# Sums moved off GpSimd in a fused attention and gated-layer kernel: the out projection's sums of h go to VectorE and ahead of their stage, its sums of C to accumulating DMAs

## The chip, the cores and the metric

One core of one Trainium2 chip. The metric is the device time of one execution in microseconds (us); lower is better. Three runs of the kernel before are given, and one further execution was profiled.

## The reference, cut to what matters

```python
def phi(x):                                   # x: 8 batches, 8 heads, 576 positions, 64
    h = einsum('bhsd,md->bhsm', x, omega) - sum(x*x, -1)/2
    return exp(h - max(h, -1)) / sqrt(128)
q_p, k_p = phi(q * 64**-0.25), phi(k * 64**-0.25)
kv  = einsum('bhsm,bhsd->bhmd', k_p, v);  z = sum(k_p, axis=2)
att = einsum('bhsm,bhmd->bhsd', q_p, kv) / (einsum('bhsm,bhm->bhs', q_p, z)[..., None] + 1e-6)
x   = att.transpose(0, 2, 1, 3).reshape(4608, 512)
xn  = x / sqrt(mean(x*x, -1) + 1e-6) * rms_g
g   = xn @ w_gate;  val = xn @ w_val          # 512 -> 1536
out = (silu(g) * val) @ w_out                 # the out projection, 1536 -> 512
```

The change concerns the last product. There h = silu(g) * val, turned so that its 1536 features lie on partitions in twelve tiles of 128 (f = 0 to 11) and its 4608 tokens along the free axis in nine blocks of 512.

## The kernel before, in words

**Stages.** Attention and normalisation come first, mixed with the gate and value products of the first three feature tiles. Then the "units" make the other nine feature tiles of h in two passes (`PASSES`); each finished 128x512 piece of h is stored to DRAM (`h_scratch`). In the second pass the blocks 6, 7 and 8 are served first (`TURNS`). The last stage is the out projection.

**The out projection in 15 products.** The nine token blocks are taken as three triples, `TRIPLES = ((6, 7, 8), (0, 1, 2), (3, 4, 5))`, called triple 0, 1 and 2 here. For a triple the work is one block product C = A B, where A is w_out cut in 2 x 3 blocks, B is h cut in 3 x 3 blocks b(j, l) (j a third of the features, that is four tiles; l a token block), and C has 2 x 3 blocks c(i, l). A bilinear scheme (`PRODUCTS`, `MADE`) makes C from 15 products where the plain way needs 18. The left operands are sums of blocks of A, made once. The right operands are sums of blocks of h, named e1 to e13 and f3: 13 sums for each triple, of which 11 are operands; e1 and e8 are only steps. For example e1 = b11 + b21, e2 = b01 - e1. The other four operands are plain blocks b. Each product's result is added to or subtracted from one or two blocks of C, 18 such readings for a triple (a "sum of C" below).

Each right operand has four feature tiles and is handled in two halves of two tiles, g = 0 and g = 1, each 128 x 1024 numbers. The loads `hb<-h_scratch` fetch a half (512 KB). A sum of h is one instruction `hb<-hb,hb` (or `he`) on 128x1024. Before the change the sums with g = 0 run on VectorE (DVE) and those with g = 1 on GpSimd (POOL):

```python
by = "POOL" if g else "DVE"
made[nm, g] = add(by, ..., form(nm, g, host, ve if by == "DVE" else nc.gpsimd), ...)
```

**Three passes for one product.** TensorE (PE) works on numbers split in a high and a low part. `halve` casts the high part on ScalarE (ACT), `hR3h<-hb`, and makes the remainder by a subtraction, `hR3l<-hb,hR3h`, on DVE (the number is that of the product, 0 to 14). The weights are split in the same way, `oh<-oraw` and `ol<-oraw,oh`, 30 halves in all, once; `oraw` comes from `wl_scratch`. Products 0 to 3 have theirs early; of the products 4 to 14 the half g = 1 has its `ol` on POOL. A product is 2 halves x 2 output tiles (u = 0, 1) x 6 matmuls of 128x512, which makes 24, and the stage 45 x 24 = 1080.

**Slots and chains.** The split operands lie in five slots (`SLOTS_R`) that are used in turn, so that half i can be cast when PE is done with half i - 5. The results are held in PSUM in seven chains; a chain that several products add to (as chain 4: products 5 and 7; chain 6: products 3, 6, 8, 11) may go on only when the earlier reading of it is done. The first reading of each block of C is a copy on ACT (`c<-q`, L1588 or L1586), each later one an addition on DVE (`c<-c,q`, L1590 and L1592), into a tile of the pool `acc` (up to nine); after the last one SP stores the tile to `out_dram`. `hb` has up to eleven buffers.

**Order.** A planner (`Plan`) simulates all instructions with estimated costs and keys and writes them out in one fixed order for each engine; each engine works through its own list in that order and waits at the head for what is not ready. SP's list holds all DMA issues, loads and stores alike.

Of the kernel before, what the change touches and what calls it, by code (L numbers as in the profile page):

```python
# [9 lines left out]
F32 = mybir.dt.float32  # L10
# [11 lines left out]
P = 128  # L22
# [58 lines left out]
    "first": {f"hb{i}": (1, 1) for i in range(8)},  # L81
    "ahead": {"k6": (1, 1), "k7": (1, 1), "k8": (1, 1), "wa": (1, 1)},
    "last": {"wo": (1, 1)},
}
# [3 lines left out]
    "hb": ("raw", 11),  # L88
# [25 lines left out]
)  # L114
WHERE = LONE + tuple(x[0] for x in LEFT)
# [185 lines left out]
def performer_glu_kernel(  # L301
# [14 lines left out]
    wl_d: bass.AP,  # L316
):
# [25 lines left out]
    def leave(group):  # L343
        stacks.pop(group).close()
# [988 lines left out]

    base = 6000
    for ps, units in enumerate(PASSES):
        if ps == len(PASSES) - 1:
            for n in range(EARLY, 3 * NF):
# [5 lines left out]
                ["ahead", "products"],  # L1343
# [17 lines left out]
    in_c = change(list(range(to_c)), ["products"], ["last"])  # L1361
# [3 lines left out]
    def out_weights(n, key):  # L1365
# [28 lines left out]
        for g in range(KT // 2):  # L1394
# [9 lines left out]
            for k in range(2) if n in (0, 12) else (None,):  # L1404
# [4 lines left out]
                else:  # L1409
# [6 lines left out]
                        "POOL" if n > 3 and g == 1 else "DVE", lambda o=out: o("h"),  # L1416
# [8 lines left out]
    def out_right(tr, key):  # L1425
# [3 lines left out]
        need = []  # L1429

        def want(nm):
            if nm in need:
                return
            if nm in MADE:
                want(MADE[nm][0])
                want(MADE[nm][2])
            need.append(nm)

        steps = []
        for n, (_, nm, _, _) in enumerate(PRODUCTS):  # L1440
            want(nm)
            steps += [x for x in need if x not in [y for y, _ in steps]] and [
                (x, None) for x in need if x not in [y for y, _ in steps]
            ]
            steps.append((nm, n))
        last = {}
        for at, (nm, n) in enumerate(steps):
            for x in (nm,) if n is not None or nm not in MADE else (nm, MADE[nm][0], MADE[nm][2]):
                last[x] = at

        def load(nm, g):
            def go():
                j, l = int(nm[1]), int(nm[2])
                t[nm, g] = tile_("hb", [P, 2, TB], f"h{nm}_{tr}_{g}")
# [5 lines left out]
        def form(nm, g, host, eng):  # L1460
            def go():
# [5 lines left out]
                eng.tensor_tensor(  # L1467
# [31 lines left out]
        soon = {}  # L1499
        for at, (nm, n) in enumerate(steps):  # L1500
            if n is None:
                soon[nm] = next(m for x, m in steps[at:] if m is not None)
        for at, (nm, n) in enumerate(steps):
            for g in range(KT // 2):
                if n is not None:
                    readers[nm, g].append(halves(n, g, nm))
                elif nm not in MADE:
                    j, l = int(nm[1]), int(nm[2])
                    f, c0 = KT * j + 2 * g, blocks[l] * TB
                    after = [  # L1510
                        i
                        for key_, i in st.items()
                        if key_[0] == "hs" and key_[1] in (f, f + 1)
                        and key_[2] < c0 + TB and key_[2] + key_[3] > c0
                    ]
                    token[nm, g] = ("hb", tr, nm, g)
                    takes.append(token[nm, g])
                    made[nm, g] = add(
                        "SP", TB / 977 / RATE, load(nm, g), after + [to_c],
                        key + 4 * soon[nm] + 2 * g - 1 + 0.01 * at, [token[nm, g]], land=LATER,  # L1520
                    )
                    readers[nm, g] = []
                else:
                    x, _, y = MADE[nm]
                    host = next((z for z in (x, y) if last[z] == at), None)
                    after = [made[x, g], made[y, g]]
                    take = []
                    if host is None:
                        token[nm, g] = ("hb", tr, nm, g)
                        takes.append(token[nm, g])  # L1530
                        take = [token[nm, g]]
                    else:
                        token[nm, g] = token.pop((host, g))
                        after += readers[host, g]
                    by = "POOL" if g else "DVE"
                    made[nm, g] = add(
                        by, 0.09 + TB / 485 if by == "DVE" else 0.25 + TB / 240,
                        form(nm, g, host, ve if by == "DVE" else nc.gpsimd),
                        after, key + 4 * soon[nm] + 2 * g - 0.5 + 0.01 * at, take,
                    )  # L1540
                    readers[x, g].append(made[nm, g])
                    readers[y, g].append(made[nm, g])
# [183 lines left out]
```

## Time and profile before

| | before |
|---|---|
| median of 3 runs | 1068.82 us (1068.14 to 1071.82) |
| the profiled execution's own time | 1072.78 us |
| its span in the profile | 1070.9 us |
| busy shares of the span | PE 96%, DVE 85%, ACT 60%, POOL 29% |
| granted PE clock, mean | 0.986 of full speed (2.4 GHz) |

The span runs from the first to the last instruction of the profiled execution. Matmuls are pipelined, so that a matmul's own duration (389 ns) is longer than the distance between two of them. "Idle" of an engine names the instruction that ended the wait.

### The profile page before, as it was taken

What the parts mean: (1) busy time and instruction counts of PE and PEld (TensorE: products, weight loads), DVE (VectorE), ACT (ScalarE), POOL (GpSimd) and SP (SyncE); (2) the same over time, 40 slices, a digit from 0 to 9 for tenths busy, and PEclk for the clock granted to TensorE, in tenths of its full rate; (3) what the DMA queues carried; (4) which work ended last, traced back from release to release, by engine and by line L of the source; (5) the groups of instructions that cost most, each with busy time, mean ns of one, the idle gap of its engine ahead of it and who ended that gap; (6) DMA issues with size and microseconds to landing.
All of it is one profiled execution on the core that took longest, in us unless ns stands there. A gap on an engine that the chain in (4) does not pass through costs nothing.

```text
span 1070.9 us, 20656 instructions
## 1 busy us (share of the span) xinstructions
PE 1030.0 (96%) x7645; PEld 872.2 (81%) x7645; DVE 911.9 (85%) x1447; ACT 647.3 (60%) x1443; POOL 314.6 (29%) x305
## 2 busy tenths in 40 slices
PE   9999999999999999999999999999998789989988
PEld 7889888888888888888897889888886668768766
DVE  5899899988887575989899677686799999999996
ACT  6999989899786465554555366445454344334431
POOL 1233212212222355000234250000156544353450
PEclk9999999999999999999999999999999989989998
DMA  7877676766543675755577464332444643453222
GB/s 250 267 235 240 216 240 217 216 207 203 165 164 109 196 227 167 272 200 187 199 239 227 155 209 139 121 118 102 174 160 125 220 168 120 142 175 118 87 91 78
DMA packets 109924, 191.37 MB, mean 179 GB/s; under 512 B 9216, under 2 KB 51968, under 8 KB 109824
## 3 DMA queue, kind: packets, MB, share of 16 engines
q1 hardware_dynamic: 109824, 190.06, 54.1%
q8 instruction: 60, 0.98, 0.4%
q14 instruction: 40, 0.33, 0.1%
HBM read 126.71 MB, written 63.31 MB: 177 GB/s over the span
## 4 chain that ended last, share of the span: by engine, by line
PE 65%; DVE 16%; ACT 6%; issue 5%; DMA 2%; POOL 0%; SPq 0%; DVEq 0%; ACTq 0%; POOLq 0%
PE pa L295 6%; PE pa L296 6%; PE pa L297 6%; PE q L296 4%; PE q L297 4%; PE q L295 4%; PE ff L295 4%; PE ff L297 4%; PE ff L296 4%; PE pb L296 3%; PE pb L295 3%; PE pb L297 3%; PE nu L842 2%; PE pjq L667 2%; PE pc L296 2%
## 5 line engine op out<-in xcount | busy, mean ns | idle before, releaser
L1467 POOL TENSOR_TENSOR hb<-hb,hb 128x1024 f32<-128x1024 f32 x33 | 97.5, 2957 | 243.0 <-DVE c L1273 123.4
L1291 ACT ACTIVATE c<-c 128x512 f32<-128x512 f32 (+1 forms) x90 | 52.8, 589 | 108.9 <-DVE c L1273 108.5
L295 PE MATMUL ff<-xhi,whi 128*128 128x512 f32 (+3 forms) x248 | 94.5, 381 | 1.5 <-ACT qpT L834 0.5
L911 POOL TENSOR_TENSOR xlo<-xr,xhi 128x256 fp32r<-128x256 f32 x72 | 55.4, 792 | 135.4 <-ACT xhi L908 135.3
L297 PE MATMUL ff<-xhi,wlo 128*128 128x512 f32 (+3 forms) x248 | 90.4, 365 | 0.0
L296 PE MATMUL ff<-xlo,whi 128*128 128x512 f32 (+3 forms) x248 | 90.3, 364 | 0.0
L697 ACT ACTIVATE qp<-pjq,biq 128x128 f32<-128x128 f32 x288 | 79.7, 411 | 16.4 <-DVE biq L688 16.3
L697 ACT ACTIVATE kp<-pjk,bik 128x128 f32<-128x128 f32 x280 | 78.6, 433 | 4.0 <-DVE bik L688 3.3
L1467 DVE TENSOR_TENSOR hb<-hb,hb 128x1024 f32<-128x1024 f32 x33 | 58.6, 1780 | 3.2 <-DMA hb<-h_scratch 2.7
L1273 DVE TENSOR_TENSOR c<-pb,u 128x512 f32<-128x512 f32 (+1 forms) x45 | 28.4, 633 | 36.2 <-PE pb L297 30.2
L295 PEld LDWEIGHTS ff<-xhi,whi 128*128 128x128 f32 x248 | 46.7, 188 | 10.3 <-ACT xr L898 0.9
L680 DVE TENSOR_REDUCE mxq<-pjq 128x4 f32<-128x512 f32 x72 | 46.6, 682 | 8.3 <-PE pjq L667 8.3
L297 PEld LDWEIGHTS ff<-xhi,wlo 128*128 128x128 f32 x248 | 46.7, 188 | 7.7
L548 POOL TENSOR_TENSOR sr<-w,w 128x256 f32<-128x256 f32 x16 | 13.9, 898 | 129.8 <-DVE w L446 129.1
L296 PEld LDWEIGHTS ff<-xlo,whi 128*128 128x128 f32 x248 | 46.8, 189 | 6.2
L680 DVE TENSOR_REDUCE mxk<-pjk 128x4 f32<-128x512 f32 x72 | 46.5, 682 | 6.0 <-PE pjk L667 6.0
L834 ACT COPY qpT<-qt 128x512 f32<-128x512 f32 x72 | 40.3, 644 | 2.7 <-PE qt L831 2.7
L667 PE MATMUL pjk<-front,ink 64*128 64x128 f32 x576 | 39.5, 279 | 1.5 <-issue 1.4
L667 PE MATMUL pjq<-front,inq 64*128 64x128 f32 x560 | 39.4, 281 | 0.5 <-DVE rec L856 0.4
L842 PEld LDWEIGHTS nu<-kv,qpT 128*64 128x64 f32 x1152 | 35.9, 137 | 4.7 <-issue 1.9
L667 PEld LDWEIGHTS pjk<-front,ink 64*128 64x128 f32 x576 | 35.5, 190 | 5.1 <-issue 2.6
L842 PE MATMUL nu<-kv,qpT 128*64 128x65 f32 x1152 | 39.5, 223 | 0.1
(289 smaller groups left out, 3383.4 us busy)
## 6 DMA issues: line engine op xcount, KB each, us to landing
hb<-h_scratch SPq DMA_DIRECT2D x54, 512.0 KB, 4.4
h_scratch<-c SPq DMA_DIRECT2D x72, 256.0 KB, 2.2
ink<-in_kx_dram SPq DMA_DIRECT2D x32, 512.0 KB, 4.9
inq<-in_qx_dram SPq DMA_DIRECT2D x32, 512.0 KB, 4.6
Xb<-xn_scratch SPq DMA_DIRECT2D x28, 512.0 KB, 4.9
f<-in_wgv_dram SPq DMA_DIRECT2D x24, 512.0 KB, 4.6
xn_scratch<-xr SPq DMA_DIRECT2D x36, 256.0 KB, 3.0
out_dram<-c SPq DMA_DIRECT2D x36, 256.0 KB, 2.1
```

The source lines that it names most:

```text
L295: nc.tensor.matmul(out, lhsT=ah, rhs=bh, start=first, stop=False, skip_group_check=again)
L296: nc.tensor.matmul(out, lhsT=ah, rhs=bl, start=False, stop=False, skip_group_check=again)
L297: nc.tensor.matmul(out, lhsT=al, rhs=bh, start=False, stop=last, skip_group_check=again)
L667: nc.tensor.matmul(t["pts"][i][:, hp, :], lhsT=x[rows, hp, :], rhs=om[rows, :], start=hp == 0 or not first, stop=True, skip_group_check=first,
L680: ve.tensor_reduce(out=by_half[:, i, :], in_=t["pts"][i], axis=AX.X, op=ALU.max)
L697: nc.scalar.activation(st[tag + "p", c][:, h, :], t["pts"][h % 2][:, h // 2, :], AF.Exp, bias=t["bi"][:, h : h + 1], scale=SCALE,)
L834: nc.scalar.copy(t["qpT"][:, 4 * half : 4 * half + 4, :], t["pt", half])
L842: nc.tensor.matmul(pt[lo:hi, i, :], lhsT=t["qpT"][:, h, lo:hi], rhs=st["kv", b][:, h, :], start=True, stop=True,)
L911: nc.gpsimd.tensor_tensor(out=st["xT", blk][1][:, ccs, cs], in0=t["xr"][:, ccs], in1=st["xT", blk][0][:, ccs, cs].bitcast(F32), op=ALU.sub ...
L1273: ve.tensor_tensor(out=t[name], in0=t[bank], in1=t[y], op=ALU.add)
L1291: nc.scalar.activation(t[nm], t[nm], AF.Silu)
L1467: eng.tensor_tensor(out=t[nm, g], in0=t[x, g], in1=t[y, g], op=ALU.add if sign == "+" else ALU.subtract,)
```

## The change

What the change does, in five parts.

1. **No GpSimd in the out projection's sums.** The 39 sums of h that POOL made, the 13 with g = 1 of each triple, are now on DVE. The 11 weight remainders `ol` with g = 1 go to DVE too.
2. **Half of triple 0's sums in the unit stage.** `staged` makes the 13 sums for the feature tiles f = 0 and 1 of each third (that is g = 0) during the second pass: 18 loads `sb<-h_scratch`, 26 sums of 128x512 on DVE and 22 stores to a new DRAM tensor `f_scratch`. In the out projection these 11 operands come by one load each (`he<-f_scratch`) and need no sum.
3. **Sums of C added in DRAM.** In triples 1 and 2, blocks of C listed in `APART` are not summed in SBUF: a reading becomes a copy on ACT into a tile of its own; the first tile is stored by SP, the following ones are sent by a DMA that POOL issues and that adds to what DRAM holds (`accum_op=ALU.add`). Such a DMA waits until the previous one on the same tile of C has landed. In triple 1 all readings of c01, c11, c02, c10 and the first of c00 and c12 are apart; in triple 2 all of c01, c11, c02 and the first of c10. In triple 0 nothing changes in this.
4. **Buffers.** `fs`, nine tiles of 128x512, serves part 2 while the units run; three of the eight later `hb` buffers therefore open only after the units' last instruction.
5. The planner's order follows from all this. PE has the same 4838 rows in the same sequence.

Counted over the whole program: DVE sums of h 39 -> 65 of 128x1024 and 0 -> 26 of 128x512; DVE sums of C 72 -> 38; ACT copies of C 36 -> 70; POOL sums of h 39 -> 0, POOL `ol` 12 -> 0, POOL DMAs 0 -> 34 of 256 KB; `hb` and `he` loads 54 -> 60.

```diff
+EARLY_F = (0, 1)
+FORMS = ("e1", "e2", "f3", "e4", "e12", "e5", "e6", "e7", "e8", "e9", "e10", "e11", "e13")
+TOLD = tuple(x for x in FORMS if x in [p[1] for p in PRODUCTS])
+APART = ({}, {"c01": 3, "c11": 3, "c02": 3, "c10": 3, "c00": 1, "c12": 1}, {"c01": 3, "c11": 3, "c02": 3, "c10": 1})
...
+    def staged(after, key):
+        blocks = TRIPLES[0]
+        for f in EARLY_F:
...
+                    ve.tensor_tensor(
+                        out=t[nm], in0=t[x], in1=t[y], op=ALU.add if sign == "+" else ALU.subtract
+                    )
...
+                return lambda: nc.sync.dma_start(f_d[TOLD.index(nm), :, f], t[nm])
...
+        if ps == len(PASSES) - 1:
+            staged(again, base - 16)
...
-                        "POOL" if n > 3 and g == 1 else "DVE", lambda o=out: o("h"),
+                        "DVE", lambda o=out: o("h"),
...
+            forms = {} if tr == 0 and 2 * g in EARLY_F else MADE
...
+                if nm in MADE:
+                    nc.sync.dma_start(t[nm, g], f_d[TOLD.index(nm), :, 2 * g : 2 * g + 2])
+                    return
...
-                    by = "POOL" if g else "DVE"
...
+                made[nm, g] = add(
+                    "DVE", 0.09 + TB / 452, form(nm, g, host), after, here - 0.5, take
+                )
...
+                if onto:
+                    nc.gpsimd.dma_start(to, t[nm, u], accum_op=ALU.add)
+                else:
+                    nc.sync.dma_start(to, t[nm, u])
...
+                    nth = [m for m, _ in parts[nm]].index(n)
+                    alone = APART[tr].get(nm, 0)
+                    begin = nth <= alone
+                    end = nth < alone or n == parts[nm][-1][0]
...
+                        onto = (nm, u) in sent
+                        sent[nm, u] = add(
+                            "POOL" if onto else "SP", 1.0 if onto else TB / 1950 / RATE,
+                            store(nm, u, onto), [sums[nm, u]] + ([sent[nm, u]] if onto else []),
+                            top, give=[("acc", tr, nm, u, begun[nm, u])], land=LATER if onto else LAND,
+                        )
```

**Place 1: DVE in triple 1, around product 8.** In the names the first number after the tile is the triple, the next is g (for `c` and `q` it is u); the long number is a buffer's. Before:

```order
L1110 TENSOR_TENSOR hR7l_0_11538<-hb_1_0_11028,hR7h_0_11537 128x1024
L1467 TENSOR_TENSOR he_1_0_11560<-hb_1_0_11391,hb_1_0_11364 128x1024
L1110 TENSOR_TENSOR hR7l_1_11558<-hb_1_1_11055,hR7h_1_11557 128x1024
L1110 TENSOR_TENSOR hR8l_0_11584<-hb_1_0_11157,hR8h_0_11583 128x1024
L1110 TENSOR_TENSOR hR8l_1_11602<-hb_1_1_11195,hR8h_1_11601 128x1024
L1592 TENSOR_TENSOR c_1_0_11366<-c_1_0_11366,q_1_0_11453 128x512
L1592 TENSOR_TENSOR c_1_1_11376<-c_1_1_11376,q_1_1_11467 128x512
```

and now:

```order
L1117 TENSOR_TENSOR hR7l_0_11673<-hb_1_0_11228,hR7h_0_11672 128x1024
L1562 TENSOR_TENSOR hb_1_0_11540<-hb_1_0_11540,hb_1_0_11629 128x1024
L1117 TENSOR_TENSOR hR7l_1_11693<-hb_1_1_11323,hR7h_1_11692 128x1024
L1562 TENSOR_TENSOR he_1_0_11716<-hb_1_0_11583,hb_1_0_11540 128x1024
L1117 TENSOR_TENSOR hR8l_0_11714<-hb_1_0_11307,hR8h_0_11713 128x1024
L1117 TENSOR_TENSOR hR8l_1_11735<-hb_1_1_11360,hR8h_1_11734 128x1024
L1117 TENSOR_TENSOR hR9l_0_11757<-he_1_0_11716,hR9h_0_11756 128x1024
L1562 TENSOR_TENSOR hb_1_1_11572<-hb_1_1_11572,hb_1_1_11718 128x1024
```

The two sums of C of product 6 are gone from DVE here, and the sums of h of both halves stand between the remainders.

**Place 2: DVE where triple 0 ends and triple 1 begins.** `hR0l` is the operand with which PE starts triple 1; the sums `c_0` are those of product 12 or 13 (`q_0_.` ending in 587, 596 and 696, 705 are product 13) and of product 14 (198, 212 and 313, 325). Before:

```order
L1592 TENSOR_TENSOR c_0_0_11169<-c_0_0_11169,q_0_0_11198 128x512
L1110 TENSOR_TENSOR ol_11242<-oraw_0_11184,oh_11232 128x512
L1592 TENSOR_TENSOR c_0_1_11173<-c_0_1_11173,q_0_1_11212 128x512
L1110 TENSOR_TENSOR hR14l_1_11227<-hb_0_1_11003,hR14h_1_11226 128x1024
L1110 TENSOR_TENSOR hR0l_0_11252<-hb_1_0_11103,hR0h_0_11251 128x1024
L1590 TENSOR_TENSOR c_0_0_11080<-c_0_0_11080,q_0_0_10587 128x512
```

and now:

```order
L1117 TENSOR_TENSOR hR14l_1_11346<-hb_0_1_11172,hR14h_1_11345 128x1024
L1562 TENSOR_TENSOR hb_1_0_11285<-hb_1_0_11285,hb_1_0_11307 128x1024
L1682 TENSOR_TENSOR c_0_0_11191<-c_0_0_11191,q_0_0_10696 128x512
L1682 TENSOR_TENSOR c_0_0_10811<-c_0_0_10811,q_0_0_10696 128x512
L1682 TENSOR_TENSOR c_0_1_11211<-c_0_1_11211,q_0_1_10705 128x512
L1682 TENSOR_TENSOR c_0_1_10824<-c_0_1_10824,q_0_1_10705 128x512
L1562 TENSOR_TENSOR hb_1_0_11285<-hb_1_0_11228,hb_1_0_11285 128x1024
L1562 TENSOR_TENSOR hb_1_1_11348<-hb_1_1_11348,hb_1_1_11360 128x1024
L1562 TENSOR_TENSOR hb_1_1_11348<-hb_1_1_11323,hb_1_1_11348 128x1024
L1684 TENSOR_TENSOR c_0_0_11191<-c_0_0_11191,q_0_0_11313 128x512
L1684 TENSOR_TENSOR c_0_1_11211<-c_0_1_11211,q_0_1_11325 128x512
L1117 TENSOR_TENSOR hR0l_0_11427<-hb_1_0_11285,hR0h_0_11426 128x1024
```

`hR0l_0` followed directly on the last remainder of triple 0; now four sums of h and six sums of C stand between them, the last two of them those of product 14.

**Place 3: DVE in the unit stage, second pass.** `sb` and `se` are the early sums, `Rb11`, `Rt1` and `Rt2` operands of the units. Before:

```order
L1110 TENSOR_TENSOR ol_9209<-oraw_0_9136,oh_9203 128x512
L1110 TENSOR_TENSOR Rb11l_9212<-Xb_9_8470,Rb11h_9211 128x2x256
L1110 TENSOR_TENSOR Rt1l_9239<-Xt_9_8690,Rt1h_9238 128x2x256
L1110 TENSOR_TENSOR ol_9209<-oraw_1_9192,oh_9203 128x512
L1110 TENSOR_TENSOR Rt2l_9261<-Xt_9_8692,Rt2h_9260 128x2x256
```

and now:

```order
L1117 TENSOR_TENSOR ol_9222<-oraw_0_9143,oh_9216 128x512
L1370 TENSOR_TENSOR sb_0_9039<-sb_0_9039,sb_0_9161 128x512
L1117 TENSOR_TENSOR Rb11l_9238<-Xb_9_8470,Rb11h_9237 128x2x256
L1370 TENSOR_TENSOR sb_0_9039<-sb_0_9186,sb_0_9039 128x512
L1370 TENSOR_TENSOR sb_0_9198<-sb_0_9198,sb_0_9039 128x512
L1370 TENSOR_TENSOR se_0_9269<-sb_0_9186,sb_0_9198 128x512
L1117 TENSOR_TENSOR Rt1l_9267<-Xt_9_8690,Rt1h_9266 128x2x256
```

The units' operands `Rb11` and `Rt1` now stand behind early sums on the same list.

## Rows read from the trace of the kernel before

**Rows 1.** The page, parts 1 and 2: the span, and the busy tenths of PE, DVE and POOL and PE's granted clock in 40 slices of 26.8 us.

```profile
span 1070.9 us, 20656 instructions
...
PE   9999999999999999999999999999998789989988
...
DVE  5899899988887575989899677686799999999996
...
POOL 1233212212222355000234250000156544353450
PEclk9999999999999999999999999999999989989998
```

**Rows 2.** Windows: busy time of each engine in stretches of the span, with granted clock, share of the DMA engines and GB/s. The last three are about the three triples.

```profile
core 0: us, PE busy (x) PEld busy (x) DVE busy (x) ACT busy (x) POOL busy (x), PEclk, DMA share, GB/s
0.00:100.00 100.00, 95.75 (x1222) 83.97 (x1223) 82.41 (x210) 88.30 (x257) 23.96 (x45) 1.00 0.78 255
...
600.00:700.00 100.00, 100.00 (x521) 86.23 (x521) 66.75 (x93) 56.97 (x109) 20.67 (x25) 1.00 0.47 153
700.00:760.00 60.00, 60.00 (x266) 49.69 (x265) 40.34 (x48) 26.73 (x40) 4.10 (x2) 1.00 0.38 134
...
780.00:883.00 103.00, 89.28 (x361) 71.63 (x360) 102.64 (x78) 47.84 (x66) 60.44 (x25) 0.93 0.52 171
883.00:975.00 92.00, 85.88 (x365) 69.71 (x364) 90.47 (x68) 36.79 (x42) 38.69 (x13) 0.96 0.41 135
975.00:1071.00 96.00, 85.96 (x362) 69.27 (x360) 83.81 (x66) 32.64 (x38) 33.45 (x11) 0.96 0.29 99
```

**Rows 3.** Waits of PE from 780 to 1071 us: who waited for whom, us in total, times, longest.

```profile
PE q L296 <- DVE hR11l L1110: 11.3, 3, 4.2
PE q L295 <- DVE c L1592: 10.5, 4, 3.2
PE q L295 <- ACT c L1588: 2.4, 1, 2.4
PE q L297 <- DVE ol L1110: 1.4, 1, 1.4
PE q L296 <- DVE hR4l L1110: 0.6, 1, 0.6
```

**Rows 4.** Timeline of PE: start, duration, and in brackets the idle time before it with what ended it. First matmuls of products 0 and 1 of triple 0, of product 0 of triple 1, of product 11 of triple 1, the wait within it, of product 12, of product 0 of triple 2, and the last matmul.

```profile
780.71 0.39 PE L295 MATMUL q<-hR0h,oh 128*128 128x512 f32 x1
...
786.15 0.39 PE L295 MATMUL q<-hR1h,oh 128*128 128x512 f32 x1
...
883.75 0.39 PE L295 MATMUL q<-hR0h,oh 128*128 128x512 f32 x1
...
946.61 0.39 PE L295 MATMUL q<-hR11h,oh 128*128 128x512 f32 x1
...
953.45 0.80 PE L296 MATMUL q<-hR11l,oh 128*128 128x512 f32 x1 [3.73 <-DVE hR11l L1110]
...
958.30 0.63 PE L295 MATMUL q<-hR12h,oh 128*128 128x512 f32 x1
...
975.15 0.39 PE L295 MATMUL q<-hR0h,oh 128*128 128x512 f32 x1
...
1066.92 0.39 PE L297 MATMUL q<-hR14h,ol 128*128 128x512 f32 x1
```

**Rows 5.** Durations by tile: minimum, median and maximum in ns, first and last start. DVE's sums of h and two of its remainders, POOL's sums of h, and DVE's sums of C.

```profile
L1467 DVE TENSOR_TENSOR hb<-hb,hb x33: 1209/1225/3416, 765.4 to 1040.2; 128x1024 f32<-128x1024 f32 x33
...
L1110 DVE TENSOR_TENSOR hR3l<-hb,hR3h x6: 1211/1213/1226, 789.5 to 988.8; 128x1024 fp32r<-128x1024 f32 x6
...
L1110 DVE TENSOR_TENSOR hR8l<-hb,hR8h x6: 1210/2846/3406, 825.6 to 1018.4; 128x1024 fp32r<-128x1024 f32 x6
...
L1467 POOL TENSOR_TENSOR hb<-hb,hb x33: 2390/3252/3382, 755.8 to 1039.2; 128x1024 f32<-128x1024 f32 x33
...
L1590 DVE TENSOR_TENSOR c<-c,q x42: 672/676/689, 813.2 to 1062.5; 128x512 f32<-128x512 f32 x42
```

**Rows 6.** Timelines of DVE and of POOL in triple 1: start, duration, instruction. Neighbours are merged (x2, x4), and the duration is then from the first start to the last end.

```profile
906.62 2.35 DVE L1110 TENSOR_TENSOR hR5l<-hb,hR5h 128x1024 fp32r<-128x1024 f32 x2
908.89 1.27 DVE L1592 TENSOR_TENSOR c<-c,q 128x512 f32<-128x512 f32 x2
...
917.39 3.10 DVE L1110 TENSOR_TENSOR hR7l<-hb,hR7h 128x1024 fp32r<-128x1024 f32 x1
920.52 3.31 DVE L1467 TENSOR_TENSOR he<-hb,hb 128x1024 f32<-128x1024 f32 x1
923.75 1.21 DVE L1110 TENSOR_TENSOR hR7l<-hb,hR7h 128x1024 fp32r<-128x1024 f32 x1
...
917.01 5.73 POOL L1467 TENSOR_TENSOR hb<-hb,hb 128x1024 f32<-128x1024 f32 x2 [12.53 <-DVE hR6l L1110]
```

**Rows 7.** Smaller pieces, from the timeline of DVE (a weight remainder and a 128x512 sum with both inputs in SBUF, POOL idle) and from the groups by line on ACT from 780 us on (count | busy us, mean ns | idle before).

```profile
587.34 0.69 DVE L1167 TENSOR_TENSOR Xt<-Xb,Xb 128x512 f32<-128x512 f32 x1
...
635.38 0.69 DVE L1110 TENSOR_TENSOR ol<-oraw,oh 128x512 fp32r<-128x512 f32 x1 [0.67 <-ACT oh L1105]
...
L1588 ACT ACTIVATE c<-q 128x512 f32<-128x512 f32 x30 | 17.1, 595 | 18.5 <-POOL ol L1110 8.2 <-PE q L297 6.4 <-DVE c L1590 3.9
```

**Rows 8.** DMA issues from 780 us on: tensors, count, KB of each, median us from issue to landing.

```profile
hb<-h_scratch SPq DMA_DIRECT2D x46, 512.0 KB, 4.3
out_dram<-c SPq DMA_DIRECT2D x36, 256.0 KB, 2.1
oraw<-wl_scratch SPq DMA_DIRECT2D x19, 256.0 KB, 3.2
```

**Rows 9.** The end of the chain that ended last: the last sum of C on DVE.

```profile
1067.35 0.69 DVE c L1592
```

More of the change, by code (lines that the diff above doesn't have):

```diff
@@ L80 @@
     "products": {"lw": (1, 1), "hB": (4, 1), "g": (4, 1)},
-    "first": {f"hb{i}": (1, 1) for i in range(8)},
+    "first": {f"hb{i}": (1, 1) for i in range(5)},
     "ahead": {"k6": (1, 1), "k7": (1, 1), "k8": (1, 1), "wa": (1, 1)},
+    "stage": {f"fs{i}": (1, 1) for i in range(9)},
     "last": {"wo": (1, 1)},
+    "more": {f"hb{i}": (1, 1) for i in range(5, 8)},
 }
@@ L1342, in performer_glu_kernel @@
                 ["products", "later"],
-                ["ahead", "products"],
+                ["ahead", "stage", "products"],
                 lambda: left_tiles(*units[1:]),
@@ L1360, in performer_glu_kernel @@
     )
-    in_c = change(list(range(to_c)), ["products"], ["last"])
+    in_c = change(list(range(to_c)), ["products", "stage"], ["last", "more"], give=[("open", nm) for nm in GROUPS["more"]])
     lo_w = {}
@@ L1498, in out_right @@
         readers, token = {}, {}
[L1499 to L1515, printed above, removed]
+        todo = sorted(
+            (m, g, at, nm, n is not None)
+            for g, (_, steps, _) in plans.items()
+            for at, (nm, n, m) in enumerate(steps)
+        )
@@ new lines, in out_right @@
+        for m, g, at, nm, final in todo:
+            forms, _, last = plans[g]
+            here = key + 4 * m + 2 * g + 0.01 * at
+            used = (nm,)
+            if final:
+                readers[nm, g].append(halves(m, g, nm))
+            elif nm not in forms:
+                if nm in MADE:
+                    after = [st["fs", nm, 2 * g], st["fs", nm, 2 * g + 1]]
+                else:
+                    after = stored(KT * int(nm[1]) + 2 * g, 2, blocks[int(nm[2])])
+                token[nm, g] = ("hb", tr, nm, g)
+                takes.append(token[nm, g])
+                made[nm, g] = add(
+                    "SP", TB / 977 / RATE, load(nm, g), after + [to_c], here - 1, [token[nm, g]],
+                    land=LATER,
+                )
+                readers[nm, g] = []
+            else:
+                x, _, y = forms[nm]
+                used = x, y
+                host = next((z for z in (x, y) if last[z] == at), None)
+                after = [made[x, g], made[y, g]]
+                take = []
+                if host is None:
@@ L1544, in out_right @@
-                for z in (nm,) if n is not None or nm not in MADE else (x, y):
-                    if last[z] == at and (z, g) in token:
-                        add("NONE", 0, lambda: None, readers[z, g], give=[token[z, g]])
+                    take = [token[nm, g]]
+                else:
+                    token[nm, g] = token.pop((host, g))
+                    after += readers[host, g]
+                made[nm, g] = add(
+                    "DVE", 0.09 + TB / 452, form(nm, g, host), after, here - 0.5, take
+                )
@@ L1651, in performer_glu_kernel @@
         out_triple(tr, base + 4 * len(PRODUCTS) * tr + 0.5)
-    add("NONE", 0, lambda: [leave(g) for g in ("banks", "last", "ahead", "first", "kept", "front", "operands", "edge")], list(range(len(plan.items))))
+    add("NONE", 0, lambda: [leave(g) for g in ("banks", "more", "last", "ahead", "first", "kept", "front", "operands", "edge")], list(range(len(plan.items))))
     plan.turns["hb"] = takes
+    plan.turns["fs"] = stages
     with tc.manual_schedule():
```

166 lines of the change are left out of this document (106 added, 60 removed).

## The prediction

> **What bounds the kernel now.** I read first where PE is not full, then who keeps it waiting, then why that engine is late.
>
> The page's tenths show PE full until about slice 30 of 40 and then with eights, and at the same place DVE at 9 and POOL at 3 to 6 [rows 1]. The windows place it: from 600 to 760 us PE is busy all the time, at full clock, while DVE has 33 of 100 and 20 of 60 us free; in the three triples DVE is busy 102.6 of 103, 90.5 of 92 and 83.8 of 96 us [rows 2]. So the loss lies in the out projection, and DVE is what is full there.
>
> How large it is follows from PE's own pace. Products 0 and 1 of triple 0 start at 780.71 and 786.15, 5.44 us apart, with no wait between; 15 products are 81.6 us and the three triples 244.8. They take 103.0, 91.4 and 92.2 us (780.71 to 883.75 to 975.15 to the end of the last matmul at 1067.3), that is 21.4, 9.8 and 10.6 more, **41.8 us in all** [rows 4]. Waits of PE make 26.2 of them, 23.8 of these for DVE [rows 3]. The other 15.6 us are matmuls at lower clock, which the trace shows behind the longer waits: product 11 of triple 1 lasts from 946.61 to 958.30, 11.69 us; 5.44 of work and 3.73 of waiting leave 2.5 us of slower matmuls, and the mean granted clock of the triples is 0.93 to 0.96 [rows 2, 4].
>
> Why is DVE full? Its sums of h and its remainders, the same shape, have two durations: 1.21 us, or up to 3.4 [rows 5]. In the timeline the long ones (3.10, 3.31) stand exactly under POOL's sums at 917.01, and the sums of C, with one input in PSUM, are 0.67 always [rows 5, 6]. So a POOL sum costs DVE 2.1 us. Triple 1 checks it: 30 remainders and 13 sums at 1.14 (two take 2.35) are 49.0, 24 sums of C at 0.60 are 14.4, together 63.4; DVE was busy 90.5; the excess, 27.1, is 13 POOL sums x 2.1 [rows 2, 6].
>
> The Trainium skill says the same in "SBUF — State Buffer", section "Who interferes with whom": a DVE instruction with two SBUF inputs contends with a GpSimd instruction that reads SBUF, and one with at most one SBUF input does not.
>
> **The change, part by part.** *POOL's sums go, DVE takes them over.* DVE's work in a triple, by the same prices, with 0.60 for a weight remainder (0.69 alone, overlapping like the sums of C) [rows 6, 7]:
> - triple 0: 30 remainders and 13 sums, 49.0; 24 sums of C, 14.4; 20 whole and four half-size `ol` after PE's start, 13.5. That is 76.9 of PE's 81.6, 94%.
> - triple 1: 56 x 1.14 = 63.8, and 4 sums of C, 2.4: 66.2, 81%.
> - triple 2: 63.8 and 10 sums of C, 6.0: 69.8, 86%.
>
> All lie under PE's time, so PE is the bound again, and up to 41.8 us come back: waits first, and the slow clock with them, since it only follows waits. The five slots let DVE run about four halves (10.9 us) ahead, enough to level the uneven products of triples 1 and 2.
>
> *A new wait where triple 0 ends.* The order puts before `hR0l_0`, with which PE starts triple 1, four sums of C of product 13, three sums of h and two sums of C of product 14 (place 2). The last of these needs PE's end of product 14: as at the end of the kernel it starts 0.4 us after the last matmul began and takes 0.69 [rows 4, 9], then the remainder takes 1.21. So PE waits at least 2.3 us. With DVE late by a microsecond or two, as 94% suggests, it is up to 4. I take 3.5, and 2.0 of slow clock behind it as at product 11 [rows 4]: **+5.5** (2.3 to 6.5). Between triples 1 and 2 no sum of product 14 stands in that place, and DVE has 15 us to spare: nothing.
>
> *Triple 0's loads.* It moved 171 GB/s x 103 us = 17.6 MB; six more loads of 512 KB make 20.7 MB, in 81.6 us 254 GB/s [rows 2, 8]. The first 100 us of the kernel ran at 255 GB/s and 0.78 of the DMA engines, so it is possible, but DVE waits at the head of its list for a late half, and it has 5 us to spare. Between 0 and all of the triple's gain (14 us beyond what is already taken back) I take **+2**, near the lower end, since loads are issued products ahead.
>
> *The early sums.* 26 sums of 128x512 at about 0.6 are 16 us on DVE [rows 7], against 53 us free from 600 to 760 [rows 2]; 40 more DMAs of 256 KB are 10 MB where 134 to 153 GB/s run. I cost them at 0. The cover goes if a sum waits for its load with a unit's operand behind it (place 3). A store that must land (2.1) and a load (3.2) [rows 8] bound one such stall at 5 us.
>
> *ACT.* 34 more copies at 0.6 are 20 us [rows 7] on 69 of 188 in triples 1 and 2 [rows 2]: 0. A copy waits for a tile of `acc`; 32 copies share nine tiles in 81.6 us, so a tile may be held 23 us on average.
>
> *POOL's 34 DMAs.* No row has a DMA issued from POOL. What it takes from DVE lies between nothing and the 2.1 us of a POOL sum; a DMA issue computes no tile, so I take 0. Until it lands, the nearest rows are a store, 2.1, and a load plus a store, 5.3 [rows 8], far below the 23 us. The last one, c10 of triple 2, is ready one product (5.4 us) before the end, and the kernel's last store goes through SP as before, 3.6 us behind the last matmul [rows 1, 4]: 0, at most 1.
>
> On that first price the same page and section say that contention needs a GpSimd instruction that reads SBUF, and infer that descriptor generation wants the write interface, so a tensor_tensor and a DMA issue would not meet. By it the price is 0 and the sum stays; by the other end, the row of a POOL sum, it is rival 2. No row shows which.
>
> **Sum.** 1070.9 - 41.8 + 5.5 + 2.0 = 1036.6 span. The profiled execution took 1072.78, 1.9 over its span, and the median of the runs is 4.0 below that (the table): 1036.6 + 1.9 - 4.0 = 1034.5, say **1035 us**, a ratio of 0.968.
>
> **The rivals.**
> 1. *Triple 0 keeps its length*: its loads or weights come late and DVE, in order, waits for them. For it: 94% of DVE and 254 GB/s. Against: the list asks for them early. Triple 0 at 103 instead of 89: +14, 1049 (1043 to 1056).
> 2. *POOL's DMAs hold DVE like its sums did*, slower than before. Triples 1 and 2 have 15.4 and 11.8 us of slack for 20 and 14 DMAs, so up to 0.8 us each costs nothing. At 2.1 us it is 42.0 - 15.4 + 29.4 - 11.8 = 44 over: 1079. It decides at 34p - 27.2 = 34, p = 1.8 us. For it: every POOL instruction of this stage does so now. Against: those read tiles, a DMA issue doesn't.
> 3. *The accumulating DMAs are slow*: an added part waits on POOL's list for its predecessor's landing, tiles of `acc` fill up, ACT's copies wait with the casts behind them. It needs more than some 12 us a landing in the bursts of four copies (products 9, 10, 13), or 4.8 us each in a row on POOL (163 us for 34). At 5.5 us each the last two triples stretch by 24 us: 1059.
> 4. *DVE's long instructions have another cause than POOL*, so that DVE does 26 more sums at the long price: no gain, about 1068. Against: rows 5 and 6 match one by one.
>
> To rival 3 speaks a box of the same page, section "SBUF: two separate sides": a DMA issued from GpSimd took some 3100 instead of 620 ns beside a DVE copy that held the shared ports. By it a landing would be an estimated 2.5 us later, which is still under 12 us and moves no term; no row here has such a DMA.
>
> **How the numbers follow.** The forecast (1027 to 1043: all comes back, or with every small term at its upper end) 0.64; rival 1 0.18; rival 2 0.07; rival 3 0.06; rival 4 0.05. A measurement of this kernel tells 0.3%, 3 us, from no change. Slower than that: rival 2 and a little of 3, 0.08. Within it: most of rival 4, 0.04. Faster: 0.88. The range, 1027 to 1054, takes in the forecast and nearly all of rival 1.
>
> **What the profile after would show.** DVE's sums and remainders all near 1.21 us from 780 us on; triples 1 and 2 near 82 us with no PE wait over 1 us; triple 0 between 82 and 86; one PE wait of 2 to 4 us for `hR0l` at the start of triple 1. PE still full from 600 to 780. Wrong would be: DVE instructions of 2 us and more beside POOL's DMAs (rival 2), ACT copies waiting for a DMA (rival 3), DVE waiting for `he`, `hb` or `oraw` in triple 0 (rival 1), a wait of PE for a unit's operand (the early sums).

## The result, and the profile after

The changed kernel takes **1031.68 us** (median of 4 runs, 1031.45 to 1032.0), the kernel before beside it 1068.48: a ratio of 0.965, 95% interval 0.963 to 0.968. A second series gave 1031.22. The profiled execution of the changed kernel took 1031.67 us, with a span of 1029.9.

The page, parts 1 and 2, against [rows 1] (one slice is now 25.7 us):

```profile
span 1029.9 us, 20788 instructions
...
PE   9999999999999999999999999999999999999998
...
DVE  5899899988986757898989948888868999879885
...
POOL 1242212121223248100202444000000000132120
PEclk9999999999999999999999999999999999999999
```

PE is full to the last slice, at full clock. The windows answer to [rows 2]: the unit stage first, then the three triples, cut at PE's first matmul of each.

```profile
core 0: us, PE busy (x) PEld busy (x) DVE busy (x) ACT busy (x) POOL busy (x), PEclk, DMA share, GB/s
600.00:700.00 100.00, 100.00 (x522) 86.27 (x521) 76.83 (x113) 56.48 (x109) 18.25 (x22) 1.00 0.69 233
700.00:760.00 60.00, 60.00 (x266) 49.69 (x265) 44.81 (x58) 28.98 (x45) 0.00 (x0) 1.00 0.54 188
778.70:860.30 81.60, 81.60 (x362) 67.58 (x360) 74.43 (x88) 46.25 (x64) 0.00 (x0) 1.00 0.73 248
860.30:943.90 83.60, 81.91 (x361) 67.51 (x360) 71.15 (x64) 48.37 (x64) 15.87 (x18) 1.00 0.84 213
943.90:1025.70 81.80, 81.78 (x361) 67.40 (x359) 63.98 (x60) 40.97 (x52) 14.02 (x16) 1.00 0.68 148
```

The triples take 81.6, 83.6 and 81.8 us instead of 103.0, 91.4 and 92.2, and DVE has 7 to 18 us free in each. From 600 to 700 and from 700 to 760 us DVE is busy 10 and 4.5 us longer than before, with the early sums, and PE is as full as it was. Of PE's waits in the whole out projection [rows 3] one is left:

```profile
PE q L302 <- DVE hR0l L1117: 1.7, 1, 1.7
```

Durations by tile from 778 us on, as in [rows 5]: DVE's sums of h, one of its remainders that had a median of 2.85 us, the DMAs that POOL issues, and the issues of DMAs, of these and of SP's stores of the same size (count, KB, median us from issue to landing).

```profile
L1562 DVE TENSOR_TENSOR hb<-hb,hb x53: 1216/1219/1226, 778.5 to 1005.5; 128x1024 f32<-128x1024 f32 x53
L1117 DVE TENSOR_TENSOR hR8l<-hb,hR8h x5: 1222/1225/1228, 817.6 to 980.3; 128x1024 fp32r<-128x1024 f32 x5
L1694 POOL DMA_DIRECT2D out_dram<-c x34: 865/870/1164, 883.8 to 1022.0; - x34
```

```profile
out_dram<-c SPq DMA_DIRECT2D x36, 256.0 KB, 2.8
out_dram<-c POOLq DMA_DIRECT2D x34, 256.0 KB, 5.0
```

No DVE instruction of this shape exceeds 1.23 us any more; a DMA issue keeps POOL 0.87 us, and its data land after 5.0 (medians).

### The profile page after: what moved, and what is told of

The parts are those of the page before. It is cut to its first block, busy times and chain, and to the rows that moved or that the text cites. A ratio compares the mean times of both kernels' runs of the same rounds, so it can differ in the third digit from the quotient of the medians.

```text
span 1029.9 us, 20788 instructions
## 1 busy us (share of the span) xinstructions
PE 1013.1 (98%) x7645; PEld 862.8 (84%) x7645; DVE 857.5 (83%) x1477; ACT 667.5 (65%) x1477; POOL 206.5 (20%) x288
## 4 chain that ended last, share of the span: by engine, by line
PE 85%; DVE 8%; ACT 5%; issue 1%; DMA 0%; POOL 0%; DVEq 0%; ACTq 0%; POOLq 0%
PE q L302 8%; PE q L303 8%; PE q L301 8%; PE pa L301 7%; PE pa L302 6%; PE pa L303 6%; PE ff L301 4%; PE ff L303 4%; PE ff L302 4%; PE pb L301 3%; PE pb L303 3%; PE pb L302 3%; PE pjk L674 2%; PE pjq L674 2%; PE nu L849 2%; PE qt L838 2%
## 5 line engine op out<-in xcount | busy, mean ns | idle before, releaser
L1694 POOL DMA_DIRECT2D out_dram<-c x34 | 29.9, 887 | 363.0 <-ACT c L1680 294.1
L1562 DVE TENSOR_TENSOR hb<-hb,hb 128x1024 f32<-128x1024 f32 x55 | 66.4, 1220 | 0.4
L1273 ACT COPY m<-pa 128x512 f32<-128x512 f32 (+1 forms) x45 | 24.2, 543 | 28.3 <-PE pa L303 28.3
L849 PEld LDWEIGHTS nu<-kv,qpT 128*64 128x64 f32 x1152 | 35.9, 137 | 4.7 <-issue 2.3
```

The lines of the kernel that those rows point to most:

```text
L849: nc.tensor.matmul(pt[lo:hi, i, :], lhsT=t["qpT"][:, h, lo:hi], rhs=st["kv", b][:, h, :], start=True, stop=True,)
L1562: ve.tensor_tensor(out=t[nm, g], in0=t[x, g], in1=t[y, g], op=ALU.add if sign == "+" else ALU.subtract,)
L1694: nc.gpsimd.dma_start(to, t[nm, u], accum_op=ALU.add)
```

## The experiments

**What was open.** The theory: the gain is PE's excess over 81.6 us a triple, and it comes back because a POOL sum, which reads SBUF, held DVE for 2.1 us while DVE's own sum costs 1.14. Rivals: the gain comes from the work that parts 2 and 3 take off DVE; DVE's long instructions had another cause; the adding DMAs cost something themselves. Twelve runs bear on this; the table gives their medians and the lengths of the three triples in their traces in us (first matmul of a triple to the first of the next, for the last to the end of its last matmul). Part numbers are those of the change.

| kernel | median us | triple 0, 1, 2 |
|---|---|---|
| before | 1068.5 to 1069.8 | 103.0, 91.4, 92.2 |
| changed | 1031.7, again 1031.2 | 81.6, 83.6, 81.8 |
| part 1 alone | 1045.5 | 89.5, 87.0, 84.7 |
| parts 1 and 2, no adding DMA | 1044.7 | 81.6, 87.9, 89.7 |
| parts 1 and 3, no early sums | 1042.6 | 91.5, 85.6, 81.8 |
| sums with g = 1 back on POOL | 1051.5 | 89.1, 91.3, 85.3 |
| changed + POOL subtractions | 1047.7 | 92.7, 87.8, 81.8 |
| changed + POOL memsets | 1032.5 | 81.6, 84.1, 81.8 |
| changed, triple 0 apart too | 1029.8 | 81.6, 81.6, 81.8 |
| changed, all apart | 1041.2 | 81.6, 86.0, 81.8 |
| no adding DMA, sums of C later in rank | 1040.1 | 81.6, 85.3, 89.1 |
| no adding DMA, sums of C behind | 1044.0 | 81.6, 86.1, 89.3 |
| changed, sums of C later in rank | 1030.9 | 81.6, 82.3, 81.8 |

**1. Does POOL's reading hold DVE?** Two kernels give POOL useless work in triple 0, where the changed kernel has none there. The edit, after each product of triple 0 (`dm` is a tile of 128x160 of its own):

```diff
+nc.scalar.copy(dm, ps[:, 0:160])              # paces POOL by the products
+for _ in range(6):
+    nc.gpsimd.tensor_tensor(out=dm, in0=dm, in1=dm, op=ALU.subtract)
```

> The changed kernel, with work for GpSimd added in triple 0, where it had none: after each of the 15 products six subtractions on a small tile of 128x160 that nothing else uses, both inputs in SBUF, let go by a small ScalarE copy at the end of the product. The results are not used. An estimate from the 128x256 remainders of GpSimd (0.73 us alone): about 0.45 us each, 2.7 us in a product, 41 us in the triple. Theory (a GpSimd instruction that reads SBUF holds a VectorE instruction with two SBUF inputs): by the ratio of the kernel before, 2.1 of 3.3 us, VectorE loses some 26 us and has 103 us of work in triple 0; total 1054 us (1044 to 1062), VectorE's 128x1024 instructions of 1.22 us stretched beside them, its sums of C still 0.68. Rival (VectorE's long instructions had another cause, such as the sums' own data): 1032 us, nothing stretched.

and with `for _ in range(11): nc.gpsimd.memset(dm, 0.0)` instead:

> The same as the kernel with GpSimd's subtractions, but the six subtractions are eleven memsets of the same 128x160 tile, which write SBUF and read nothing; about 0.22 us each, 2.4 us in a product. Theory (it is the reading that collides): no VectorE instruction is stretched, total 1032 us (1031 to 1034). Rival (any GpSimd work on SBUF holds VectorE): stretched instructions as with the subtractions, 1045 us or more.

1047.7 us with the subtractions (2 runs), 1032.5 with the memsets. Durations by tile, subtractions first (POOL's own, DVE's sums of h, weight remainders, sums of C), then memsets:

```profile
L1710 POOL TENSOR_TENSOR dm<-dm x88: 452/782/1378, 786.4 to 879.4; 128x160 f32<-128x160 f32 x88
L1562 DVE TENSOR_TENSOR hb<-hb,hb x10: 1209/1468/1472, 779.4 to 865.8; 128x1024 f32<-128x1024 f32 x10
L1117 DVE TENSOR_TENSOR ol<-oraw,oh x24: 518/936/975, 785.6 to 863.5; 128x512 fp32r<-128x512 f32 x20, 128x256 fp32r<-128x256 f32 x4
L1682 DVE TENSOR_TENSOR c<-c,q x14: 673/676/687, 810.1 to 869.1; 128x512 f32<-128x512 f32 x14
```

```profile
L1710 POOL MEMSET dm<- x165: 231/233/239, 785.9 to 865.4; 128x160 f32 x165
L1562 DVE TENSOR_TENSOR hb<-hb,hb x13: 1214/1217/1227, 778.9 to 859.6; 128x1024 f32<-128x1024 f32 x13
L1117 DVE TENSOR_TENSOR ol<-oraw,oh x24: 417/682/692, 785.2 to 852.0; 128x512 fp32r<-128x512 f32 x20, 128x256 fp32r<-128x256 f32 x4
```

Beside reading, a DVE instruction with two SBUF inputs is mostly 0.25 us longer (1.22 to 1.47, 0.68 to 0.94), and one with an input in PSUM keeps its 0.676. Beside 165 memsets nothing changes, although the same ACT copies pace them (they keep POOL busy for 35.9 us of triple 0, the subtractions for 72.2). So the mechanism is shown, with data that have nothing to do with the sums. Its price I had wrong (1047.7 lies in the forecast range, but 6 us under the 1054 forecast): I scaled by POOL's busy time, but DVE pays the same 0.25 us for an instruction of 1.22 as for one of 0.68, and POOL's instructions are stretched too (0.45 at the least, 0.78 in the median, up to 1.38). Who starts first matters: a remainder of DVE that began at 829.76, ahead of POOL's subtraction at 829.96, kept its 1.21 us, and the subtraction took 1.33. That fits a lock that one instruction holds from start to end: 0.25 us of waiting for one of 0.45, 2.1 for one of 2.4. The Trainium skill says so in "SBUF — State Buffer", section "SBUF: two separate sides": the port pair that DVE and GpSimd share is an exclusive lock, which the one that starts first holds for the whole instruction. The traces agree, with the 1.21 and 1.33 us above.

**2. The parts by themselves.** Part 1 alone is the kernel before with

```diff
-"POOL" if n > 3 and g == 1 else "DVE"
+"DVE"
...
-by = "POOL" if g else "DVE"
+by = "DVE"
```

> The kernel before, with the first part of the change alone: GpSimd's sums of h, and its share of the weight remainders, are made by VectorE; nothing is made early and nothing is added in DRAM. Theory (a GpSimd sum takes 2.1 us from VectorE, VectorE's own sum only 1.14): VectorE's work by the prices of the prediction is 92.9, 79.4 and 75.9 us in the three triples, so triple 0 is 11 us longer than TensorE's 81.6 and the two others full or nearly so. Total 1045 us (1042 to 1052), that is some 24 us of the 37 come from this part alone; no VectorE sum or remainder over 1.3 us. Rival (VectorE is simply short of capacity, and the gain comes from the work that the early sums and the DMAs take off it): with 13 more sums VectorE is fuller than before, so 1068 us or slower.

1045.49 us, as the theory said, and two thirds of the gain (24 of 38 us) from giving DVE twice the sums of h. Where the time lies was not foreseen as well: over 81.6 us the triples are 7.9, 5.4 and 3.1 us long, where the prices give 11 for the first and little for the others. The rival is refuted for these 24 us alone; the other 13.8 come only with parts 2 and 3. The reverse puts the sums back into the changed kernel (`by = "POOL" if g else "DVE"`, and `nc.gpsimd` for them):

> The changed kernel, with the sums of h of every second half given back to GpSimd; the early sums, the DMAs and the weight remainders on VectorE stay. Theory (each GpSimd sum blocks VectorE for 2.1 us): VectorE's own work is 66.6, 52.6 and 50.3 us, and 13 sums x 2.1 = 27.3 come on top in triples 1 and 2, somewhat fewer in triple 0, so 93.9 at most, 79.9 and 77.6. Total 1043 us (1036 to 1050), with VectorE sums and remainders of 2 to 3.4 us back in the trace. Rival (moving work to an engine that has 80 of 100 us free only helps): VectorE has 15 to 31 us of slack in each triple, the wait at the start of triple 1 goes, total 1030 us.

1051.51 us: slower by 20 than the changed kernel, where the rival's count of free time promised a gain. The order of size is right, but the time lies above the forecast range (1036 to 1050), 8 us over the 1043 forecast. The timeline of POOL and then of DVE in triple 1 shows the cost that was forecast and one that was not:

```profile
936.41 9.35 POOL L1562 TENSOR_TENSOR hb<-hb,hb 128x1024 f32<-128x1024 f32 x3
951.25 1.78 POOL L1695 DMA_DIRECT2D out_dram<-c  x2 [5.49 <-DVE c L1685]
952.46 3.01 POOL L1562 TENSOR_TENSOR hb<-hb,hb 128x1024 f32<-128x1024 f32 x1
```

```profile
936.60 3.62 DVE L1117 TENSOR_TENSOR hR13l<-hb,hR13h 128x1024 fp32r<-128x1024 f32 x1
940.14 6.70 DVE L1562 TENSOR_TENSOR hb<-hb,hb 128x1024 f32<-128x1024 f32 x2
```

DVE's instructions beside POOL's sums take 3.3 to 3.6 us again; and POOL, in order, stands 5.49 us before a DMA whose part of C is not ready, with a sum of h behind it. That second cost I had not counted; that it makes up the 8 us is not shown.

Without the early sums (`EARLY_F = ()`):

> The changed kernel, with no sum of h made early: triple 0 makes all of them. Theory: VectorE has 91.8 us of work in triple 0, 10.2 more than TensorE, and 65.6 and 66.8 in the others. Total 1042 us (1040 to 1048), triple 0 at 92 us or a little more, the two others at 82 to 84; nothing changes from 600 to 780 us. Rival (the early sums' loads and stores cost something where they are made): the start of the out projection comes earlier by that cost, and the total is under 1040.

1042.62 us, triple 0 91.5, as worked out (triple 1, at 85.6, is over its 82 to 84); the early sums themselves cost nothing (in the changed kernel PE stays full from 600 to 760 us). Without the adding DMAs (`APART = ({}, {}, {})`):

> The changed kernel, with all sums of C made by VectorE again and no DMA that adds in DRAM. Theory: VectorE's work is 76.9, 81.8 and 75.9 us in the triples against TensorE's 81.6; triple 1 is at its edge, the two others keep their length. Total 1032 to 1037 us, most likely 1034, so the DMAs are worth 0 to 5 us. Rival (GpSimd's DMAs carry a cost of their own on VectorE or on the DMA queues): 1029 to 1031, faster than the changed kernel.

1044.68 us: my 1034 was far off. So the parts don't add. Beside part 1, the early sums alone bring 0.8 us and the DMAs alone 2.9, the first well within the 4 us by which the runs of each of these kernels scatter; both together bring 13.8. The table shows where it goes: the early sums shorten triple 0 from 89.5 to 81.6, but triple 2, whose work they don't touch, grows from 84.7 to 89.7.

**3. Why the DMAs are worth 13 us.** By work alone triple 2 without them has 75.9 us for DVE, and was busy 76.1 in a triple of 89.7. Most of DVE's waits there (10.0 of 12.9 us) stand before sums of C, and 6.8 of 9.1 in triple 1. Part 1 alone has the same instructions in triple 2 and took 84.7. One place in both, the timeline of DVE before product 10 of triple 2, first without the adding DMAs, then part 1 alone:

```profile
1000.64 0.69 DVE L1682 TENSOR_TENSOR c<-c,q 128x512 f32<-128x512 f32 x1 [0.22 <-PE q L303]
1005.35 0.69 DVE L1684 TENSOR_TENSOR c<-c,q 128x512 f32<-128x512 f32 x1 [4.01 <-ACT c L1678]
1005.95 1.22 DVE L1117 TENSOR_TENSOR hR10l<-hb,hR10h 128x1024 fp32r<-128x1024 f32 x1
```

```profile
1008.20 0.69 DVE L1590 TENSOR_TENSOR c<-c,q 128x512 f32<-128x512 f32 x1 [0.67 <-PE q L297]
1008.80 1.22 DVE L1110 TENSOR_TENSOR hR10l<-hb,hR10h 128x1024 fp32r<-128x1024 f32 x1
1010.06 1.23 DVE L1467 TENSOR_TENSOR hb<-hb,hb 128x1024 f32<-128x1024 f32 x1
```

In the first, a sum of C of product 9 stands ahead of `hR10l`; DVE idles 4.01 us, by the profile for ACT's copy of the same result, which itself began at 1004.72, when PE had ended that part of product 9, and PE then waits for the remainder (product 10 takes 6.82 us instead of 5.44). In the second only sums of product 8 stand there, the remainder is done 3 us before product 9 ends at 1013.4, and product 10 takes 5.44. The order differs because the planner laid it anew. This place is one of several: of the 14.35 us that triples 1 and 2 lose over PE's pace without the DMAs, 2.9 fall on the two products 10, 5.8 on the two products 0 and 4.8 on products 12 and 13. I tried to change the order alone, first by the planner's rank, so that a sum of C no longer goes ahead of all else but with the remainders of two products later (`top if begin else key + 4 * (n + 2)`):

> The kernel without DMAs that add (all sums of C on VectorE), with one thing changed: a sum of C no longer goes ahead of all else on VectorE's list as soon as its product ends, it is ranked with the remainders of two products later. VectorE's work is the same, 76.9, 81.8 and 75.9 us. Theory (the 13 us that this kernel lost against the changed one came from VectorE standing idle ahead of sums of C whose product TensorE had not ended, 9.1 us in triple 1 and 12.9 in triple 2, not from their work): those waits go, the triples come back to 82 to 85 us, total 1034 us (1031 to 1038). Rival (the sums' work itself is too much for VectorE): 1042 to 1047 us as before.

then by a dependence, so that it follows both remainders of the next product (`after.append(st["RO", tr + (n == 14), (n + 1) % 15, 1])`):

> The kernel without DMAs that add, with another order on VectorE: a sum of C of product n stands behind both remainders of product n+1. The rank given in the earlier trial left the sums of product 9 ahead of the first remainder of product 10; here they come after it. Work is the same, 76.9, 81.8 and 75.9 us. Theory (what was lost against the changed kernel is VectorE standing before sums whose product TensorE has not ended, while TensorE then waits for the remainder behind them): TensorE's waits for the remainders of product 10 go, the triples take 82 to 84 us, total 1035 us (1032 to 1038). Rival (the sums' work is too much): VectorE idles no more than 3 us in triples 1 and 2 and they still take 85 us and more, total 1039 to 1045 us.

1040.11 and 1043.95 us: the theory's 1034 and 1035 are missed. The first lies between theory and rival and is no test of this place, since the sums of product 9 still stand ahead of `hR10l` and DVE still waits 2.9 us before them. The second lies where the rival put it, but not with the rival's sign, a DVE that idles at most 3 us. DVE no longer waits for that sum, but for ACT, whose list has a copy of the same product ahead of the cast (triple 1, ACT and then DVE):

```profile
914.11 0.59 ACT L1678 COPY c<-q 128x512 f32<-128x512 f32 x1 [4.90 <-PE q L303]
914.60 1.05 ACT L1112 CAST hR10h<-hb 128x1024 fp32r<-128x1024 f32 x1
```

```profile
915.68 1.23 DVE L1117 TENSOR_TENSOR hR10l<-hb,hR10h 128x1024 fp32r<-128x1024 f32 x1 [4.02 <-ACT hR10h L1112]
```

What is shown: at these places DVE idles behind something that waits for PE, while PE's next operand is queued behind it. What stays open: why triples 1 and 2 together lose 11 to 14 us over PE's 163.2 in all three orders without the DMAs. By the prices of the prediction (1.14 a sum or remainder, 0.60 a sum of C) DVE's need is uneven: for products 6 to 14 and the next triple's product 0 it is an estimated 59.9 us without the DMAs, against 54.4 of PE's time, and 50.3 with those of triple 1. That would explain some 5 us a triple, but no run isolates it.

**4. The wait that was left.** At the start of triple 1, PE's timeline (last matmul of product 14, then product 0) and DVE's:

```profile
860.06 0.39 PE L303 MATMUL q<-hR14h,ol 128*128 128x512 f32 x1
860.29 0.39 PE L301 MATMUL q<-hR0h,oh 128*128 128x512 f32 x1
862.37 0.50 PE L302 MATMUL q<-hR0l,oh 128*128 128x512 f32 x1 [1.69 <-DVE hR0l L1117]
```

```profile
859.78 1.40 DVE L1684 TENSOR_TENSOR c<-c,q 128x512 f32<-128x512 f32 x2
861.09 2.36 DVE L1117 TENSOR_TENSOR hR0l<-hb,hR0h 128x1024 fp32r<-128x1024 f32 x2
```

Two edits take the sums of product 14 from ahead of it: `APART[0] = {"c00": 3, "c10": 3}`, eight more DMAs,

> The changed kernel, with triple 0's readings of c00 and c10 also kept apart and added in DRAM, so that VectorE makes no sum of C after product 12 of triple 0, and the first remainder of triple 1 follows two sums of h. Theory (the wait of 1.7 us at the start of triple 1 comes only from the sums of C of products 13 and 14 that stand ahead of that remainder): the wait goes, product 0 of triple 1 takes 5.44 instead of 7.46 us, total 1029.7 us. Rival (VectorE is late there by its 94% of triple 0): a wait of at least 1 us stays, 1031 us or more.

and, with no more DMAs, the rank of the trial above in the changed kernel:

> The changed kernel with the same DMAs, and the sums of C ranked with the remainders of two products later, which puts the first remainder of triple 1 ahead of the two sums of product 14 (three sums of product 13 still stand ahead of it). Theory (that remainder waits for the end of product 14 only because those two sums stand ahead of it): TensorE's wait there goes or falls under 0.7 us, total 1030 us (1029.5 to 1030.8). Rival (it is late for VectorE's 94%): the wait stays above 1 us, 1031.5 us.

The first has no PE wait left in the out projection and takes 1029.79 us (ratio to before 0.963, 0.961 to 0.964), the fastest kernel here. The second waits 0.4 us and takes 1030.94 against 1031.22 for the changed kernel beside it; its triples are 1.3 us shorter, but its profiled out projection began 2.1 us later, at 779.8 instead of 777.7, and by its runs the two kernels can't be told apart.

> The changed kernel once more, unaltered, beside the three others of this call, so that differences of two microseconds can be read: 1031.7 us, one wait of TensorE, 1.7 to 2.2 us, at the start of triple 1.

**5. More DMAs still.** All later readings apart, in all triples:

> The changed kernel, with every later reading of C kept apart and added in DRAM in all three triples: no sum of C on VectorE, 72 DMAs from GpSimd instead of 34. Theory: VectorE has 64.9, 65.0 and 63.8 us of work and nothing on its list that waits for the end of a product, the three triples take 81.6 us each; the wait of 2.0 us at triple 1 goes, and the end of the kernel gets longer by about 2 us, as its last part of C now lands by an adding DMA (5.0 us in the changed kernel) instead of a sum and a store (0.7 and 2.8). Total 1032 us (1029 to 1035). Rival (the adding DMAs, or GpSimd issuing them, are the next limit): ScalarE's copies wait for tiles of acc, TensorE waits for them, 1038 us or more.

1041.22 us instead of the 1032 forecast, in the rival's range but mainly by another way than the rival's (ACT's copies wait 4.9 us in all for a landing). The windows of the first two triples have the DMA engines full in the first:

```profile
778.55:860.15 81.60, 81.60 (x361) 67.45 (x360) 59.19 (x64) 56.54 (x85) 16.78 (x19) 1.00 1.00 298
860.15:946.17 86.02, 82.55 (x362) 67.53 (x362) 71.12 (x62) 52.66 (x70) 21.73 (x25) 1.00 0.97 233
```

and DVE and POOL show what follows, at the end of triple 0 and at the kernel's end:

```profile
856.47 2.48 DVE L1562 TENSOR_TENSOR hb<-hb,hb 128x1024 f32<-128x1024 f32 x2 [3.67 <-DMA hb<-h_scratch]
```

```profile
1026.84 0.86 POOL L1694 DMA_DIRECT2D out_dram<-c  x1 [1.96 <-DMA out_dram<-c]
1029.16 0.86 POOL L1694 DMA_DIRECT2D out_dram<-c  x1 [1.46 <-ACT c L1680]
1030.79 0.88 POOL L1694 DMA_DIRECT2D out_dram<-c  x1 [0.77 <-DMA out_dram<-c]
```

At 1.00 of the DMA engines a half for triple 1 comes late (a load `hb<-h_scratch` lands after 7.2 us in the median instead of 5.7, and product 0 takes 9.86), and the last additions queue for their predecessors' landing: the last matmul ends at 1027.93, the span at 1037.5, 9.6 us behind it instead of 4.2. Rival 3 of the prediction asked for more than 12 us a landing before the adding DMAs decide anything. Here 72 of them make the kernel 10 us slower at a landing of 6.0, through a load beside them and through the kernel's end.

## Why the prediction was right, point by point

- **PE's excess of 41.8 us comes back**: right. The triples sum to 247.0 us against 286.6 before, where 244.8 is PE's own pace; the granted clock is 1.00 in all three, so the slow matmuls went with the waits.
- **The mechanism and its 2.1 us**: right. The two kernels with useless POOL work show the mechanism, the sums given back show the size (3.35 and 3.62 us instead of 1.22), and part 1 alone shows that it pays.
- **"All lie under PE's time, so PE is the bound again"**: true here, but not for the reason given alone. Without the adding DMAs 75.9 us of work in triple 2 also lie under PE's 81.6, and the triple takes 89.7. That the order of the lists leaves no such waits in the changed kernel was worked out only for the ends of the triples; for the rest of them it was in part luck.
- **DVE's work by prices** (76.9, 66.2, 69.8): busy 74.4, 71.2, 64.0, together 209.6 instead of 212.9; some of it is done a triple earlier than I counted (88, 64 and 60 instructions instead of 91, 60 and 66).
- **The new wait, +5.5**: right place, mis-sized; it costs 2.0 us. The lower bound of 2.3 was the time from the last matmul's start to the remainder's end, which the rows give as 862.37 - 860.06 = 2.31; but the last matmul itself (0.23) and the first of product 0, which needs only the high part (0.39), lie within it, and 1.69 is left. DVE was not late: its last sum of product 14 began at 860.49 (861.18 less 0.69), just behind that matmul's end at 860.45. And one wait of 1.69 us brought no slow clock: the next products take 5.44.
- **Loads of triple 0, +2**: nothing; 248 GB/s, triple 0 is 81.60 us. Early sums, ACT's copies and POOL's DMAs at nothing: right. The margin of the DMAs is thinner than it looks, as 72 of them show.
- **The end**, 0: +0.6 (4.2 us behind the last matmul instead of 3.6); stores land in 2.8 instead of 2.1 in the median.
- **Not foreseen**: the first matmul of the out projection starts at 778.7 instead of 780.7. Of these 2.0 us 1.6 stand already at the first matmul of the units (385.26 instead of 386.83), ahead of the first early load at 607.6. The other kernels' out projections started between 777.7 and 779.8, so this is scatter, and the profiled execution of the kernel before was a late one.
- **From span to median, -4.0**: this step failed. It took the profiled execution's lead over the median as a constant; the new profiled execution lies on its median. The span, forecast 1036.6, came out at 1029.9, 6.7 lower (1070.9 - 41.8 + 2.2 - 2.0 + 0.6); the forecast median was only 2.8 too high because this error covers 4.0 of it, which is luck.

Rival 2, that POOL's DMAs hold DVE like its sums did, is refuted: DVE's instructions beside 34 of them stay at 1.22 us. The Trainium skill ("SBUF — State Buffer", section "Who interferes with whom") says that a DVE instruction with two SBUF inputs contends with a GpSimd instruction that reads SBUF, not with one that only writes it. The memsets (1.217 us beside them) and the subtractions (1.47) agree.

## What to carry to other kernels

Before work is shared between DVE and POOL, look whether DVE's two-SBUF-input instructions grow beside POOL's: here with twice the sums of h on DVE the kernel was faster by 24 us, since a sum on the helper cost DVE more (2.1 us) than making it (1.14). A sum of work per stage is not enough for engines with fixed lists: an instruction that waits for the end of a product, ahead of the operand of the next, can cost more than its duration (4.01 us of idle time for a sum of 0.69), and whether one stands there can change whenever a planner lays the list anew. Parts of a change that relieve different stages of one engine may each seem worth little until all are in.

## What the runs showed of the hardware

In the two sizes tried, the cost to a DVE instruction with two SBUF inputs follows the length of the POOL instruction that reads beside it, 0.25 us for one of 0.45 and 2.1 for one of 2.4, not POOL's busy share. A DMA that adds 256 KB to DRAM took POOL 0.87 us and landed in 5.0 us, against 2.8 for a plain store through SP; with 72 of them in the kernel the DMA engines were full in triple 0, at 298 GB/s, and the landing rose to 6.0, that of the plain stores to 4.9.
